# Mish in two instructions instead of one, shorter ends, and a new instruction order

## The chip, the cores and the metric

The kernel runs on one core of a Trainium2 chip. TensorE (PE), VectorE (DVE), ScalarE (ACT), GpSimd (POOL) and the DMA queues of SyncE (SP) and ScalarE work side by side and meet at semaphores. The metric is the time of one execution on the device in microseconds; lower is better.

## The reference

One input x of 2048 rows and 640 columns goes through two branches that a gate mixes row by row: full softmax attention with 32 heads of 20 columns, and a dense layer with Mish.

```
g = sigmoid((x * gate_w).sum(-1, keepdims=True))
qkv = x @ wqkv                       # 640 -> 3 * 640, 32 heads of 20
p = softmax(q @ k^T * 20**-0.5)      # 2048 x 2048 for each head
a = (p @ v) @ wo
h = x @ w1 + b1                      # 640 -> 1536
b = (h * tanh(log1p(exp(-|h|)) + max(h, 0))) @ w2     # Mish, 1536 -> 640
out = g * a + (1 - g) * b
```

The inputs are bfloat16.

## The kernel before

**Groups and units.** Attention runs in 32 groups: four heads (one row group of PE for each) by 512 queries. A group has 16 sets, one for each block of 128 keys, and a set has four units, one for each head. A unit is one score matmul (`score`, L1262): 32 x 128 keys against 32 x 512 queries, into one PSUM bank. So there are 2048 units.

**Two ways to an exponential.** Most sets go to ScalarE: `emit_exp` (L1312) takes the banks of two or three units in one instruction and writes to the ring `E`. Some sets go to VectorE instead (the planner calls one such set `d`): `power_of` (L473) makes a power of two from each bank by one multiply-add into 16-bit integers, and two further copies of the set, moved by whole numbers (`SHIFT`), are added up with fitting factors `VD` to better the approximation. These copies are made by VectorE (`shift`, L604, one instruction) or by GpSimd (`part`, L572, four instructions). The products with the values (`emit_pv`, L1355) gather into one bank, `acc`, with a column of ones for the row sums. At a group's end `normalise` transposes that bank (L1376), takes reciprocals (L1390), multiplies on GpSimd (L1397) and sends the result through DRAM.

**The other work.** Products that must be done some time during the attention are *chains* with a start and a due time: the q, k and v products (`xT,ws`, `wv,xT`), h = x @ w1 (`h_chain`, evacuated with the bias at L891), the Mish products (`b_chain`, `w_sb,big`) and the product with wo (`wo_chain`, `wo_sb,od`, evacuated at L1064). All of them go out through line L637, four column tiles side by side.

**Mish.** The hidden layer is done in two batches of 1024 rows. `mish` (L909 to L925) counts the finished pairs of h and then queues one ScalarE instruction over 12288 elements a partition. Exp and Mish need different tables, so each batch has a table load before it and one after it. A b product of the batch may begin when the instruction is done (`act_ready`).

**Who sets the order.** The schedule is fixed when the program is built. A planner keeps a model clock for each engine, and at each step lets `step_pe`, `step_act`, `step_dve` and `step_pool` choose the next instruction by rules (`rule`), whose settings change as the work advances (`PLAN`). The program then runs on the chip in just this order on every engine, and semaphores hold an engine where data are not there yet. At most two exps are under way at a time (`NOUT`), and seven banks are shared by scores and chains.

**Heat.** `heat`, in `step_pe`, lets the planner's PE pass one matmul's time when its recent activity is low. It emits no instruction.

**Start.** Before the loop the first 512 rows of x are loaded and transposed (L1454), `wkp` and `wqp` are put together from the loaded weights (`w_first`, `w_top`), and the first k and q are made (L1478), each into one bank, from which VectorE copies one half and ScalarE the other (L1486, L1487).

**End.** After the loop the last four row blocks get the rest of their product (L1830) and are copied out by ScalarE (L1845, L1852) and VectorE (L1854), and stored by SP's queue (L1848, L1856).

Of the kernel before, what the change touches and what calls it, by code (L numbers as in the profile page):

```python
# [9 lines left out]
P = 128  # L10
ACT = mybir.ActivationFunctionType
# [44 lines left out]
SWITCH = 100.0  # L56
# [8 lines left out]
def kernel(  # L65
# [249 lines left out]
    for u in range(NU):  # L315
        eng = nc.sync if u % 2 == 0 else nc.scalar
        eng.dma_start(out=xs[0][:, u, :], in_=x2d[u * P : (u + 1) * P, :])
    load_first(1, nc.sync)
    load_first(0, nc.scalar)
    nc.sync.dma_start(out=w_top[:, :, :], in_=wrows[:, :, D + KTOP : 2 * D])  # L320
    nc.scalar.dma_start(out=wv0[:, :, 0 : 4 * DH], in_=wrows[:, :, 2 * D : 2 * D + 4 * DH])

# [68 lines left out]
    pool_q = []  # L391
    two_port = [0.0]
    seq = [0]
    free = {"PE": 0.0, "ACT": 0.0, "DVE": 0.0, "POOL": 0.0}
# [514 lines left out]
    def mish(m, t):  # L909

        h_left[m] -= 1
        if h_left[m]:
            return
        lo = (m * MB % 2) * (FT // 2)
        v = big[:, lo : lo + MB * FT // 2, :].rearrange("p a b -> p (a b)")

        def done(t):
            for c in range(m * MB, m * MB + MB):
                for k in range(FT // 2):
                    act_ready[(c, k)] = t  # L920

        act_q.append((
            t, 2.0 * TABLE + 100.0 + MB * FT * 427.0,
            lambda t: nc.scalar.activation(v, v, ACT.Mish), done,  # L924
        ))  # L925

# [442 lines left out]
    def normalise(G, ready):  # L1369
# [3 lines left out]

        def a(t):
            st["T1"] = work.tile([P, NS, 32], F32, tag=f"T1_{i}", name="T1")
            nc.vector.transpose(out=st["T1"][:, :, :].rearrange("p b r -> p (b r)"), in_=acc[:, :])  # L1376
# [31 lines left out]
        def ends(t):  # L1408
            st["O"] = work.tile([P, QC], BF16, tag=f"O{i}", name="O")
            for h in range(2):  # L1410
                q = slice(h * QC // 2, (h + 1) * QC // 2)
                b_ = slice(h * NS // 2, (h + 1) * NS // 2)
                nc.vector.tensor_tensor(
                    out=T2[i][:, q].rearrange("p (b r) -> p b r", r=32)[:, :, 0:DH],
                    in0=st["T1"][:, b_, 0:DH],
                    in1=st["rec"][:, b_].unsqueeze(2).to_broadcast([P, NS // 2, DH]),
                    op=ALU.mult,
                )
                nc.vector.transpose(out=st["O"][:, q], in_=T2[i][:, q])
            o_last[p] = st["O"]  # L1420

        def c_done(t):
# [49 lines left out]
    pad_copy(nc.vector, wqp, w_first[0][:, :, :])  # L1472
    sb = [bank_ap(g, [P, QC]) for g in (6, 2)]
    kT[0] = kTb[0]
    qT[0] = qTb[0]
    for w, dst, k in ((wkp, kT[0][:, 0:QC], 0), (wqp, qT[0][:, :], 1)):
        for kt in range(KT):
            nc.tensor.matmul(  # L1478
                sb[k][:, :],
                lhsT=w[:, kt, :, :].rearrange("p h d -> p (h d)"),  # L1480
                rhs=xT[:, kt, 0:QC],
                start=(kt == 0),
                stop=(kt == KT - 1),
            )
        h_ = QC // 2
        nc.vector.tensor_copy(out=dst[:, 0:h_], in_=sb[k][:, 0:h_])  # L1486
        nc.scalar.copy(out=dst[:, h_:QC], in_=sb[k][:, h_:QC])  # L1487
    for p in range(NQ - NSB, NQ):
# [72 lines left out]
    work_log = deque()  # L1561
    heats = [0]

# [8 lines left out]
    def step_pe(t):  # L1572
# [34 lines left out]
        def go_f():  # L1607
# [4 lines left out]
            return sw + cost  # L1612

        def heat(room):

            cost = switch("V") + MM
            if pv_G[0] >= NG or acc_free[0] > t or activity(t) > rule.HEAT or not pv_done[pv_G[0]]:
                return None
            if cost + SWITCH + rule.HROOM > room:
                return None  # L1620
            enter("V")
            note(t, MM, 1.0)
            heats[0] += 1
            return cost

# [91 lines left out]
        if mode[0] in ("V", "F") and slack < rule.SWTH and not (stuck_ or end):  # L1717
            return d_alone(rule.DQ3) or heat(room)
        if n_pv and (n_pv >= rule.VMIN or tight or last_of_group) and (
# [5 lines left out]
        if n_pv and (n_pv >= rule.VMIN or tight or last_of_group or end):  # L1725
            return go_v()
        return d_alone(rule.DQ4) or heat(room)

# [11 lines left out]
    def step_dve(t):  # L1740
        best = None
        for it in dve_q:
            if it[1] <= t and (it[6] is None or it[6](t)):
                due = it[1] + (WAIT0, rule.WAIT1, rule.WAIT2, MWAIT)[it[0]]
# [99 lines left out]
    for u in range(2):  # L1844
# [3 lines left out]
        nc.sync.dma_start(out=rows_[u], in_=ots_[u][:, :])  # L1848
    for u, half, eng in ((2, 0, 0), (2, 1, 0), (3, 0, 0), (3, 1, 1)):
        dst, src = ots_[u][:, half * HALF : (half + 1) * HALF], places[u][half][:, 0:HALF]  # L1850
        if eng:
            nc.scalar.copy(out=dst, in_=src)  # L1852
        else:
            nc.vector.tensor_copy(out=dst, in_=src)  # L1854
        if half:
            nc.sync.dma_start(out=rows_[u], in_=ots_[u][:, :])  # L1856
    if DEBUG:
        print("model end us", t / 1e3, "last exp", last_exp[0] / 1e3, {k: v / 1e3 for k, v in idle.items()}, "sets", sum(n_d), n_d, "heats", heats[0])

# [29 lines left out]
```

## Time and profile before

Three runs took 721.22, 722.08 and 722.51 us.

| | us |
|---|---|
| median of the runs | 722.08 |
| the profiled execution | 722.37 |
| its span, first to last instruction | 720.6 |
| ACT busy | 700.0 |
| PE busy | 704.9 |
| DVE busy | 631.6 |
| POOL busy | 418.1 |
| exps on ScalarE, 710 instructions, busy | 668.8 |
| Mish, 2 instructions, busy | 20.9 |
| first score | 10.20 |
| end of the last exp | 711.85 |

Busy time is the union of an engine's instructions. Matmuls overlap and their ends are modelled, so PE's 98% says less than the starts of its instructions do. The mean of one exp is larger than the time from one exp to the next, since exps overlap as well.

The chain that ended last is made up of PE for 66% of the span and of ACT for 25%; by line, exps 24%, scores 23%, chains 21%, value products 21%. It changes between the two engines all the time: a score round waits for banks that an exp sets free, and an exp waits for a score round.

### The profile page before, as it was taken

The page shows a single profiled execution, that of the slowest core. Times are in us where ns is not written, and L with a number is a line of the kernel's source. Part 1 is how long each engine was busy: PE and PEld are TensorE (multiplying, and loading weights), DVE is VectorE, ACT ScalarE, POOL GpSimd, SP SyncE. Part 2 cuts the span into 40 slices and gives each one's busy share as a digit, 9 for nine tenths or more (in the row PEclk, how much of TensorE's full clock was granted, in tenths as well). Part 3 has the DMA queues.
Part 4 walks back from the last instruction along what each step waited for, and adds up shares of the span by engine and source line. Part 5 has one row for each costly group of instructions (what it writes and reads, how often), then busy time and mean ns, then how long its engine had stood idle before and what let it go on. Part 6 is the DMA issues. An engine that isn't in the chain of part 4 may idle for free.

```text
span 720.6 us, 24680 instructions
## 1 busy us (share of the span) xinstructions
PE 704.9 (98%) x10262; PEld 230.7 (32%) x10262; DVE 631.6 (88%) x1062; ACT 700.0 (97%) x726; POOL 418.1 (58%) x669
## 2 busy tenths in 40 slices
PE   7999999999999999999999999999989999999997
PEld 3433332222222333333333222222223333333333
DVE  4499998968868889999999998999998989999996
ACT  6899999999999999999999999999989999999996
POOL 2002864557868776877676687867964486762000
PEclk9999999999999999999999999999989999999999
DMA  9611122132322211111230223212211131131301
GB/s 249 180 24 33 31 47 52 34 69 57 80 43 51 50 29 17 23 32 28 46 92 25 46 51 84 65 43 43 60 20 30 33 68 27 31 63 15 61 20 47
DMA packets 123312, 37.86 MB, mean 53 GB/s; under 512 B 90880, under 2 KB 122640, under 8 KB 123200
## 3 DMA queue, kind: packets, MB, share of 16 engines
q1 hardware_dynamic: 121600, 35.76, 22.8%
q8 instruction: 80, 1.31, 0.8%
q10 hardware_dynamic: 1600, 0.53, 0.3%
q14 instruction: 32, 0.26, 0.2%
HBM read 22.29 MB, written 11.48 MB: 47 GB/s over the span
## 4 chain that ended last, share of the span: by engine, by line
PE 66%; ACT 25%; issue 5%; DVE 2%; DMA 1%; SPq 0%; POOL 0%; DVEq 0%; ACTq 0%
ACT E L1312 24%; PE Sp L1262 23%; PE Sp L637 21%; PE Sp L1355 21%; DVE T L473 1%; ACT big L924 1%; DMA w_top<-in_A_wqkv_dram 1%; PE Sp L1830 0%; DMA qT<-q_dram 0%; PE Sp L1478 0%; DVE T L604 0%; DMA q_dram<-st 0%; ACT L1312 0%; ACT L924 0%; DVE st L741 0%
## 5 line engine op out<-in xcount | busy, mean ns | idle before, releaser
L1312 ACT ACTIVATE E<-Sp 128x1024 bf16<-128x1024 f32 x710 | 668.8, 1079 | 6.8 <-PE Sp L1262 6.4
L572 POOL TENSOR_TENSOR T<-T,step_t 128x256 int32<-128x256 int32 x624 | 389.3, 659 | 108.0 <-PE Sp L1355 83.4
L473 DVE TENSOR_SCALAR T<-Sp 128x512 int16<-128x512 f32 (+1 forms) x595 | 391.9, 686 | 52.4 <-PE Sp L1262 46.3
L1262 PE MATMUL Sp<-qT,kT 32*128 32x512 bf16 x2048 | 288.3, 385 | 6.4 <-ACT E L1312 1.8
L1262 PEld LDWEIGHTS <-kT 32*128 32x128 bf16 x2048 | 74.2, 91 | 264.2 <-issue 260.0
L1355 PE MATMUL Sp<-E,VA 128*21 128x512 bf16 x1448 | 138.2, 383 | 0.0
L1397 POOL TENSOR_TENSOR T<-T,rec 128x320 bf16<-128x320 f32 x31 | 24.6, 792 | 164.9 <-DVE rec L1390 140.8
L604 DVE TENSOR_SCALAR T<-T 128x2048 int16<-128x2048 int16 x144 | 117.2, 819 | 1.4 <-PE Sp L1355 0.4
L1355 PE MATMUL Sp<-T,VD 128*21 128x512 bf16 x1200 | 113.5, 383 | 1.3 <-DVE T L604 1.3
L637 PE MATMUL Sp<-w_sb,big 128*32 128x320 bf16 x1536 | 79.4, 306 | 0.0
L637 PE MATMUL Sp<-xT,w1t 128*32 128x512 bf16 x960 | 76.6, 383 | 0.0
L1355 PEld LDWEIGHTS <-VA 128*21 128x21 bf16 x2048 | 45.2, 90 | 74.9 <-issue 67.3
L1355 PE MATMUL Sp<-T,VA 128*21 128x512 bf16 x600 | 58.2, 384 | 0.0
L637 PE MATMUL Sp<-xT,ws 128*32 128x512 bf16 x720 | 54.8, 382 | 0.2 <-DVE T L473 0.2
L637 PEld LDWEIGHTS <-big 128*32 128x32 bf16 x1536 | 34.8, 96 | 28.1 <-issue 18.5
L1355 PEld LDWEIGHTS <-VD 128*21 128x21 bf16 x1200 | 28.9, 90 | 37.5 <-issue 32.7
L891 DVE TENSOR_SCALAR big<-Sp,b1f 128x512 bf16<-128x512 f32 x48 | 35.6, 741 | 0.5 <-PE Sp L637 0.2
L637 PE MATMUL Sp<-wv,xT 128*32 128x81 bf16 (+2 forms) x960 | 33.0, 258 | 1.0 <-DVE T L473 1.0
L637 PE MATMUL Sp<-wo_sb,od 128*32 128x320 bf16 (+1 forms) x608 | 32.6, 302 | 0.0
L637 PEld LDWEIGHTS <-w1t 128*32 128x32 bf16 x960 | 19.6, 94 | 26.3 <-issue 21.2
L741 DVE CAST st<-Sp 128x512 bf16<-128x512 f32 x36 | 24.4, 681 | 3.8 <-PE Sp L637 3.3
L1376 DVE STREAM_TRANSPOSE T<-Sp 128x512 f32<-128x512 f32 x32 | 22.7, 709 | 2.1 <-PE Sp L1355 1.8
(74 smaller groups left out, 198.2 us busy)
## 6 DMA issues: line engine op xcount, KB each, us to landing
w1t<-in_B_w_dram SPq DMA_DIRECT2D x24, 320.0 KB
q_dram<-st SPq DMA_DIRECT2D x20, 128.0 KB
out_dram<-ot SPq DMA_DIRECT2D x16, 160.0 KB
qT<-q_dram SPq DMA_DIRECT2D x124, 20.0 KB
o_dram<-T SPq DMA_DIRECT2D x120, 20.0 KB
kT<-k_dram SPq DMA_DIRECT2D x28, 80.0 KB
k_dram<-st SPq DMA_DIRECT2D x16, 128.0 KB
big<-in_A_x_dram SPq DMA_DIRECT2D x3, 640.0 KB
```

What stands on the lines that cost most here:

```text
L473: nc.vector.tensor_scalar(out=dst.bitcast(I16), in0=src, scalar1=inv_sqrt_dh * LOG2E * 128.0, scalar2=127.0 * 128.0 + BETA, op0=ALU.mult, ...
L572: nc.gpsimd.tensor_tensor(out=tile_[:, :].bitcast(I32)[:, k * n : (k + 1) * n], in0=d["T"][:, :].bitcast(I32)[:, k * n : (k + 1) * n], in1 ...
L604: nc.vector.tensor_scalar(out=tile_[:, :].bitcast(I16), in0=d["T"][:, :].bitcast(I16), scalar1=float(SHIFT[i]), scalar2=None, op0=ALU.add,)
L637: nc.tensor.matmul(out_[k : k + 32], lhsT=lhsT[:, k : k + 32], rhs=rhs, tile_position=(0, k), **kw)
L741: nc.vector.tensor_copy(out=res["st"][:, :], in_=ps[:, :])
L891: nc.vector.tensor_scalar(out=big[:, slot.tag, (ft % 2) * QC : (ft % 2 + 1) * QC], in0=ps[:, :], scalar1=b1f[:, ft : ft + 1], scalar2=None ...
L924: lambda t: nc.scalar.activation(v, v, ACT.Mish), done,
L1262: nc.tensor.matmul(ps_cols, lhsT=kT[p][32 * t_ : 32 * t_ + 32, j * P : (j + 1) * P], rhs=qT[G][32 * t_ : 32 * t_ + 32, :], tile_position=( ...
L1312: nc.scalar.activation(E[:, x : x + n, :], ps, ACT.Exp, scale=inv_sqrt_dh,)
L1355: nc.tensor.matmul(acc[32 * t_ : 32 * t_ + DH + 1, :], lhsT=lhsT, rhs=rhs, start=(pv_done[G] == 0), stop=(pv_done[G] == pv_total[G] - 1), ...
L1376: nc.vector.transpose(out=st["T1"][:, :, :].rearrange("p b r -> p (b r)"), in_=acc[:, :])
L1397: nc.gpsimd.tensor_tensor(out=T2[i][:, :].rearrange("p (b r) -> p b r", r=32)[:, :, 0:DH], in0=st["T1"][:, :, 0:DH], in1=st["rec"][:, :].u ...
```

## The change

It has four parts.

- **Mish.** Each batch becomes two instructions of 512 rows (6144 elements a partition), one behind the other. The planner takes the first half's results as there one half earlier, and the b products of those 512 rows may be placed then.
- **The start.** `w_top` is loaded by ScalarE's queue as its third load, ahead of the q weights; the first v weights go to SP's queue in its place. The first k and q products are made in two halves of 256 columns, in banks 1 and 4, and 5 and 0, so that VectorE and ScalarE copy from different banks.
- **The end.** While the last group is normalised (`closing`), VectorE takes only work of the highest kind. Of the last copies ScalarE makes three whole row blocks and VectorE the two halves of the other; the stores keep their order.
- **The planner.** `heat` is taken out. The rules and `PLAN` are the same; since the costs of Mish and the steps differ, the planner comes to another order of the instructions on all engines after the first two groups.

```diff
+    nc.scalar.dma_start(out=w_top[:, :, :], in_=wrows[:, :, D + KTOP : 2 * D])
     load_first(0, nc.scalar)
-    nc.sync.dma_start(out=w_top[:, :, :], in_=wrows[:, :, D + KTOP : 2 * D])
-    nc.scalar.dma_start(out=wv0[:, :, 0 : 4 * DH], in_=wrows[:, :, 2 * D : 2 * D + 4 * DH])
+    nc.sync.dma_start(out=wv0[:, :, 0 : 4 * DH], in_=wrows[:, :, 2 * D : 2 * D + 4 * DH])
...
-        lo = (m * MB % 2) * (FT // 2)
-        v = big[:, lo : lo + MB * FT // 2, :].rearrange("p a b -> p (a b)")
+        one = 200.0 + FT * 427.0
 
         def done(t):
+            for k_, c in enumerate(range(m * MB, m * MB + MB)):
+                for k in range(FT // 2):
+                    act_ready[(c, k)] = t - TABLE - (MB - 1 - k_) * one
+
+        def run(t):
             for c in range(m * MB, m * MB + MB):
-                for k in range(FT // 2):
-                    act_ready[(c, k)] = t
-
-        act_q.append((
-            t, 2.0 * TABLE + 100.0 + MB * FT * 427.0,
-            lambda t: nc.scalar.activation(v, v, ACT.Mish), done,
-        ))
+                lo = (c % 2) * (FT // 2)
+                v = big[:, lo : lo + FT // 2, :].rearrange("p a b -> p (a b)")
+                nc.scalar.activation(v, v, ACT.Mish)
+
+        act_q.append((t, 2.0 * TABLE + MB * one, run, done))
...
+            closing[0] = G == NG - 1
...
             o_last[p] = st["O"]
+            closing[0] = False
...
-    sb = [bank_ap(g, [P, QC]) for g in (6, 2)]
-    for w, dst, k in ((wkp, kT[0][:, 0:QC], 0), (wqp, qT[0][:, :], 1)):
+    h_ = QC // 2
+    for w, dst, two in ((wkp, kT[0], (1, 4)), (wqp, qT[0], (5, 0))):
         for kt in range(KT):
-            nc.tensor.matmul(
-                sb[k][:, :],
-                lhsT=w[:, kt, :, :].rearrange("p h d -> p (h d)"),
-                rhs=xT[:, kt, 0:QC],
-                start=(kt == 0),
-                stop=(kt == KT - 1),
-            )
-        h_ = QC // 2
-        nc.vector.tensor_copy(out=dst[:, 0:h_], in_=sb[k][:, 0:h_])
-        nc.scalar.copy(out=dst[:, h_:QC], in_=sb[k][:, h_:QC])
+            for h in range(2):
+                nc.tensor.matmul(
+                    allb[:, two[h], 0:h_],
+                    lhsT=w[:, kt, :, :].rearrange("p h d -> p (h d)"),
+                    rhs=xT[:, kt, h * h_ : (h + 1) * h_],
+                    start=(kt == 0),
+                    stop=(kt == KT - 1),
+                )
+        nc.vector.tensor_copy(out=dst[:, 0:h_], in_=allb[:, two[0], 0:h_])
+        nc.scalar.copy(out=dst[:, h_:QC], in_=allb[:, two[1], 0:h_])
...
-        def heat(room):
-
-            cost = switch("V") + MM
-            if pv_G[0] >= NG or acc_free[0] > t or activity(t) > rule.HEAT or not pv_done[pv_G[0]]:
-                return None
-            if cost + SWITCH + rule.HROOM > room:
-                return None
-            enter("V")
-            note(t, MM, 1.0)
-            heats[0] += 1
-            return cost
...
-            return d_alone(rule.DQ3) or heat(room)
+            return d_alone(rule.DQ3)
...
-        return d_alone(rule.DQ4) or heat(room)
+        return d_alone(rule.DQ4)
...
-            if it[1] <= t and (it[6] is None or it[6](t)):
+            if it[1] <= t and (it[0] == 0 or not closing[0]) and (it[6] is None or it[6](t)):
...
-    for u, half, eng in ((2, 0, 0), (2, 1, 0), (3, 0, 0), (3, 1, 1)):
-        dst, src = ots_[u][:, half * HALF : (half + 1) * HALF], places[u][half][:, 0:HALF]
-        if eng:
-            nc.scalar.copy(out=dst, in_=src)
-        else:
-            nc.vector.tensor_copy(out=dst, in_=src)
-        if half:
-            nc.sync.dma_start(out=rows_[u], in_=ots_[u][:, :])
+    nc.scalar.copy(
+        out=ots_[3][:, :].rearrange("p (a c) -> p a c", a=2), in_=allb[:, 6:8, 0:HALF]
+    )
+    for half in range(2):
+        nc.vector.tensor_copy(
+            out=ots_[2][:, half * HALF : (half + 1) * HALF], in_=places[2][half][:, 0:HALF]
+        )
+    for u in (2, 3):
+        nc.sync.dma_start(out=rows_[u], in_=ots_[u][:, :])
```

More of the change, by code (lines that the diff above doesn't have):

```diff
@@ L392 @@
     two_port = [0.0]
+    closing = [False]
     seq = [0]
@@ L1561 @@
     work_log = deque()
-    heats = [0]
     def note(t, cost, weight):
@@ L1848 @@
         nc.sync.dma_start(out=rows_[u], in_=ots_[u][:, :])
-    for u, half, eng in ((2, 0, 0), (2, 1, 0), (3, 0, 0), (3, 1, 1)):
-        dst, src = ots_[u][:, half * HALF : (half + 1) * HALF], places[u][half][:, 0:HALF]
-        if eng:
-            nc.scalar.copy(out=dst, in_=src)
-        else:
-            nc.vector.tensor_copy(out=dst, in_=src)
-        if half:
-            nc.sync.dma_start(out=rows_[u], in_=ots_[u][:, :])
+    nc.scalar.copy(
[7 more added lines that the diff above has]
+        nc.sync.dma_start(out=rows_[u], in_=ots_[u][:, :])
     if DEBUG:
-        print("model end us", t / 1e3, "last exp", last_exp[0] / 1e3, {k: v / 1e3 for k, v in idle.items()}, "sets", sum(n_d), n_d, "heats", heats[0])
+        print("model end us", t / 1e3, "last exp", last_exp[0] / 1e3, {k: v / 1e3 for k, v in idle.items()}, "sets", sum(n_d), n_d)
 _INS = ['A_x', 'A_wqkv', 'A_wo', 'B_x', 'B_w1', 'B_b1', 'B_w2', 'gate_w']
```

## The prediction

> **What bounds the kernel now.** I read the page's engine line first, then ACT's groups with their shapes kept apart.
>
> ```profile
> span 720.6 us, 24680 instructions
> ...
> PE 704.9 (98%) x10262; PEld 230.7 (32%) x10262; DVE 631.6 (88%) x1062; ACT 700.0 (97%) x726; POOL 418.1 (58%) x669
> ...
> PEclk9999999999999999999999999999989999999999
> ```
>
> ```profile
> L1312 ACT ACTIVATE E<-Sp 128x1024 bf16<-128x1024 f32 x682 | 635.5, 1061 | 6.8 <-PE Sp L1262 6.4
> L1312 ACT ACTIVATE E<-Sp 128x1536 bf16<-128x1536 f32 x28 | 42.2, 1507 | 0.0
> L924 ACT ACTIVATE big<-big 128x12288 bf16<-128x12288 bf16 x2 | 20.9, 10444 | 0.0
> L924 ACT ACT_TABLE_LOAD x2 | 2.6, 1283 | 0.0
> ```
>
> Two engines are full, ACT and PE. Between the first exp at 10.62 us and the end of the last at 711.85, ACT stands visibly idle for only 6.8 us. Exps overlap: five in a row take 4.69 us in the timeline at 235.62, so one starts (4.69 - 1.06) / 4 = 0.907 after the other. By the same overlap of 0.154 a three-bank exp costs 1.507 - 0.154 = 1.35. ACT's own work there is 682 x 0.907 + 28 x 1.35 + 20.9 + four table loads 5.1 = 682, against 701 elapsed; some 19 us are waiting, most in lags too short to count as idle. PE is read from its starts:
>
> ```profile
> 305.78 0.39 PE L1262 MATMUL Sp<-qT,kT 32*128 32x512 bf16 x3
> 306.10 0.59 PE L637 MATMUL Sp<-w_sb,big 128*32 128x320 bf16 x12
> 306.62 0.39 PE L1262 MATMUL Sp<-qT,kT 32*128 32x512 bf16 x3
> ```
>
> A score round costs 0.32 until the column-tiled work begins. That work streams four tiles side by side: 12/4 x 320 columns at 2.4 a ns = 0.40, then 0.12 passes before the next round. Summed so from first to last score of the program, PE needs about 677 of 699 us. Neither engine has room of more than 3%, so both sums must be taken for the changed order too.
>
> **The place the change aims at** is the second Mish. Timeline of ACT, then of PE, then windows (us from:to, length, PE busy, PEld, DVE, ACT, POOL, granted clock, DMA share, GB/s):
>
> ```profile
> 519.98 10.44 ACT L924 ACTIVATE big<-big 128x12288 bf16<-128x12288 bf16 x1
> 530.44 1.28 ACT L1312 ACT_TABLE_LOAD   x1
> 531.74 1.94 ACT L1312 ACTIVATE E<-Sp 128x1024 bf16<-128x1024 f32 x2
> 535.27 1.02 ACT L1312 ACTIVATE E<-Sp 128x1024 bf16<-128x1024 f32 x1 [1.60 <-PE Sp L1262]
> 536.67 3.94 ACT L1312 ACTIVATE E<-Sp 128x1024 bf16<-128x1024 f32 x4 [0.38 <-PE Sp L1262]
> ```
>
> ```profile
> 526.33 0.40 PE L1355 MATMUL Sp<-T,VD 128*21 128x512 bf16 x4 [1.31 <-DVE T L604]
> ...
> 532.58 2.06 PE L637 MATMUL Sp<-w_sb,big 128*32 128x320 bf16 x28
> ```
>
> ```profile
> 526.20:529.60 3.40, 2.85 (x17) 0.74 (x17) 3.40 (x7) 3.40 (x1) 0.00 (x0) 0.99 0.11 39
> 529.60:533.00 3.40, 3.18 (x21) 0.70 (x23) 3.40 (x7) 3.37 (x4) 2.90 (x5) 0.50 0.22 15
> 533.00:536.40 3.40, 3.40 (x46) 1.14 (x34) 2.25 (x4) 1.70 (x2) 3.29 (x5) 0.50 0.15 9
> ```
>
> While ACT runs Mish no b product may start, the ready work runs out, and PE is left with single scores paced by DVE: 17 matmuls in the 3.4 us from 526.2, where the window after 536.4 has 60. From 529.6 to 536.4 the granted clock is 0.50. The first b products after Mish, 28 of them, then take 2.06 us instead of 28/4 x 0.133 + 0.12 = 1.05, and ACT waits 1.60 + 0.38 = 2.0. The first Mish (241.6) has no such loss: clock 1.00, busy PE, exp directly behind the table load.
>
> On that clock the Trainium skill (TensorE: Matmul & The Clock Gate, "Why this matters for your kernels") says that gaps without matmuls should stay under about 3 us, since one idle window puts the gate back to half rate. Here it fell though the longest gap was 1.31 us: sparse work was enough, so the measurement decides. By the page's rule a PE with such gaps would keep its clock, and the 2.0 us below would be no gain of a denser PE.
>
> **The change part by part**, against the profiled execution: 722.37 us, span 720.6 and 1.8 around it. The median of the runs is 722.08, 0.29 less; I take that off at the end.
>
> 1. *Start.* The last chain before the first score is:
>
> ```profile
> 6.60 0.22 DVE L1469 COPY wkp<-w_top 128x240 bf16<-128x240 bf16 x1 [0.55 <-DMA w_top<-in_A_wqkv_dram]
> 9.31 0.42 DVE L1486 CAST qT<-Sp 128x256 bf16<-128x256 f32 x1 [0.72 <-PE Sp L1478]
> 9.77 0.37 ACT L1487 CAST qT<-Sp 128x256 bf16<-128x256 f32 x1 [0.78 <-DVE qT L1486]
> 10.20 0.40 PE L1262 MATMUL Sp<-qT,kT 32*128 32x512 bf16 x4 [0.99 <-ACT qT L1487]
> ```
>
> The halves of k and q now lie in different banks, and in the changed program ACT's copy waits for PE only: 9.77 - 9.31 = 0.46 saved. w_top goes from fourth on SP's queue (issued 2.12) to third on ACT's (such an issue stood at 1.65): 0.47 earlier at most; nothing if the transfers still end together. Moved behind it, the q weights come perhaps 1 us later, but their copy is first needed some 1.2 us after the k product starts, which covers it; uncovered they would take the 0.47 back. What takes the place on SP's queue (the first v weights, 100 instead of 60 KB) delays the next x block by some 0.3 us; its transposes began at 10.53, after its landing. Twenty 256-column matmuls stream as many columns as ten of 512: between 0 and 0.2 more. Sum -0.9 (from -0.4 to -1.0). The first two groups stand in the same PE order afterwards, so it is carried on.
>
> 2. *Mish split.* Two more instructions; a 128x1 activation took 0.20, so 0 to 0.2 each: +0.4 of ACT. No table load is added (five before, five after), because no exp lies between the halves. The gain is in the second batch: the changed order gives PE, from the first half on, 48 and then 52 b products, a quarter of 0.133 each, so 1.6 and 1.7 us of dense work inside the second half, and an exp's scores are already there behind the table load. Work before them: 18 column-tiled steps of 0.22 and some rounds, about the 6.6 us of table load and half a Mish. So -2.0; between 0 (the wait returns) and -2.6 (the two lags after it too).
>
> 3. *The new order.* Both programs' instructions counted: exps of two banks 682 -> 693, of three 28 -> 23, of one 0 -> 1; score rounds 717 -> 711; column-tiled matmuls 8092 -> 8076; power sets on DVE 150 -> 148; shifts on DVE 144 -> 133, on POOL 156 -> 163 sets. ACT: 11 x 0.907 - 5 x 1.35 + 0.46 (half a two-bank exp; none in the trace; 0.2 to 0.9 by the 128x1 form and the two-bank one) + 0.4 = +4.1. PE: -6 x 0.44 - 16/4 x 0.213 = -3.5. DVE -8 x 0.60 - 11 x 0.68 = -12, hidden in its 90 us of idle; POOL +28 x 0.66 = 18, in its 300. The removed heat step emitted no instruction, so it costs nothing by itself.
>
> These sums are not spread evenly. Up to the last group (units 0 to 1983 of 2048) ACT has 657.2 -> 663.6, PE 654.9 -> 655.6; that stage took 677.1 before (10.2 to 687.3). Taking in each stretch of rounds the larger of the two sums, and averaging over where the cuts lie:
> stretches of 6 rounds: 676.7 -> 676.2; of 10: 672.1 -> 672.6; of 20 (a group): 667.0 -> 668.4; of 80: 662.0 -> 664.8.
> Ten is my choice: it leaves 5.0 of the 677.1 for waits outside both sums, and the trace names some 4 (2.0 after Mish; 0.6 behind a q load at 117; 0.8 on DVE at 42.3; about 0.5 at 430). So +0.5, from -0.5 (6 rounds) to +6.4 (all of ACT's sum). The other waits I take as replaced by as many.
>
> 4. *Last group.* From its first score to the closing transpose it took 712.36 - 687.3 = 25.1. Now ACT has 21.2, PE 19.4 to its last score, but DVE, packed until 707 before, has 23.5 up to its last shift, plus 0.5 for the product behind it: 24.0 if packed, 25.3 with a wait like the 1.45 before. I take 24.6: -0.5 (-1.1 to +0.2).
>
> 5. *Closing.* Other evacuations are held back during the last normalisation: the one at 712.99 put the reciprocal 0.36 later; -0.4. The copies at the very end now stand two on DVE, three on ACT. Third on ACT would end about 1.9 after the first starts; SP issues the four stores 0.47 apart from 0.7 on, so the fourth at 2.1 hides it. Without that cover it costs 0.2.
>
> Sum: -0.9 - 2.0 + 0.5 - 0.5 - 0.4 = -3.3; 722.37 - 3.3 - 0.29 = **718.8**.
>
> **Rivals.**
> *ACT's sum comes through.* If PE is no longer what is late, each stretch costs what ACT has: +6.4 instead of +0.5, so 724.7. It is one mechanism, ScalarE from group 2 to 30, and decides from the point where PE's rounds leave exps always ready. For: ACT is 97% busy and gets the larger sum over long stretches. Against: in most groups before, the elapsed time was within 0.3 of the larger sum and that was PE's more often than ACT's. Slower.
> *The wait moves.* The clock falls again, or a q load or a shift is late elsewhere by as much: 718.8 + 2.0 = 720.8, no change. For: during the first half PE still has single scores paced by DVE at 0.6 each. Against: this thin spell lasts some 3 us, before it lasted 8; and b products follow.
> *The order fits better.* Short waits shrink too: by stretches of 6, whose sum nearly reaches the 677.1, -0.5 in place of +0.5, with the last group at -1.1 and 0.6 for the q load gone: 716.6.
> *The split does nothing*, the b products stand behind other work and begin after both halves: the order counted above speaks against it; it would give 720.8 as well, and is counted with the second.
>
> **Numbers.** Forecast 0.50 (own range 717.3 to 720.6), ACT's sum 0.16, the wait moves 0.20, fits better 0.14. About 0.2%, 1.4 us, is what a measurement here tells from no change: faster is under 720.6, slower over 723.5. Faster 0.47 + 0.14 + a third of 0.20 = 0.67; slower 0.12 from ACT's sum (the rest of it falls short of 723.5); same 0.21. The range 715.8 to 723.8 leaves out most of ACT's case above 723.8 and a little below.
>
> **What would show it.** Right: the first score at about 9.3; granted clock 1.00 through the second Mish and an exp within 0.2 behind its table load; group 31 DVE packed to its end; reciprocal directly behind the closing transpose. Wrong: idle of ACT behind score rounds well over 6.8 us; a clock of 0.50 in the middle; or ACT starting exps 0.907 apart nearly throughout while the time grows.

## The result, and the profile after

The changed kernel takes 724.63 us (median of 6 runs, 723.72 to 725.96), the kernel before, run beside it, 722.30 (6 runs, 721.22 to 722.95). The ratio is 1.0032, with a 95% interval from 1.0017 to 1.0047: some 2.3 us slower. Forecast were 718.8 and 3.3 us faster. In the profiled executions the span went from 720.6 to 723.2.

The page of the changed kernel, then ACT's groups with their shapes kept apart:

```profile
span 723.2 us, 24705 instructions
...
PE 706.3 (98%) x10256; PEld 232.5 (32%) x10256; DVE 619.6 (86%) x1042; ACT 704.3 (97%) x735; POOL 430.4 (60%) x697
...
PEclk9999999999999999999999999999999999999999
```

```profile
L1315 ACT ACTIVATE E<-Sp 128x1024 bf16<-128x1024 f32 x693 | 644.4, 1064 | 6.2 <-PE Sp L1265 5.9 <-PE Sp L1358 0.2
L1315 ACT ACTIVATE E<-Sp 128x1536 bf16<-128x1536 f32 x23 | 34.2, 1487 | 0.1
L926 ACT ACTIVATE big<-big 128x6144 bf16<-128x6144 bf16 x4 | 21.1, 5315 | 0.0
```

In this execution the clock is whole up to the last matmul, where before it dipped in the middle (in two of the six runs the mean clock is 0.997 instead of 0.999, about one fall of 3.4 us at 0.50). Nothing on this page looks worse, and both busy shares stand as they were. Where the time went is seen only by stage. A group (64 units) is counted from the first score round that holds no score of the group before:

| us | before | after | the stage's change | forecast |
|---|---|---|---|---|
| first score | 10.2 | 9.2 | -1.0 | -0.9 |
| group 1 | 39.7 | 40.7 | +2.0 | 0 |
| group 5 | 126.1 | 126.7 | -0.4 | } |
| group 23 (second Mish) | 511.5 | 515.8 | +3.7 | } -1.5 |
| group 24 | 543.7 | 546.6 | -1.4 | } together |
| group 31 (the last) | 687.3 | 692.2 | +2.0 | } |
| closing transpose | 712.4 | 715.5 | -1.8 | -0.5 |
| end of the span | 720.6 | 723.2 | -0.5 | -0.4 |

(-1.5 is -2.0 for the Mish and +0.5 for the order.) A round can straddle two groups, so a stage holds some scores more or fewer: group 23 holds 67 before and 63 after, groups 24 to 30 hold 445 and 449. At about 0.34 us a score (561.2 us for 1662) that is 1.4 us, as much as the -1.4 of group 23. Over groups 1 to 30 the two kernels differ by one score. So two stages lost: the first group, and the long stretch of groups that holds neither end nor the second Mish.

**The second Mish does what was forecast.** Windows in its second half, then ACT's timeline:

```profile
528.10:531.50 3.40, 3.17 (x39) 1.08 (x35) 3.40 (x6) 3.40 (x1) 3.40 (x7) 1.00 0.41 58
531.50:535.00 3.50, 3.46 (x100) 2.55 (x100) 2.39 (x4) 3.50 (x2) 3.44 (x6) 1.00 0.13 20
```

```profile
531.58 5.31 ACT L926 ACTIVATE big<-big 128x6144 bf16<-128x6144 bf16 x1
536.91 1.28 ACT L1315 ACT_TABLE_LOAD   x1
538.20 4.69 ACT L1315 ACTIVATE E<-Sp 128x1024 bf16<-128x1024 f32 x5
```

PE has 39 and then 100 matmuls in the second half, at clock 1.00, and five exps follow the table load without a wait.

**The first group loses the start again.** SP's queue after, then before (start, length of the issues, count):

```profile
19.83 4.44 SPq L1500 DMA_DIRECT2D o_dram<-wo  x4
24.38 5.14 SPq L708 DMA_DIRECT2D k_dram<-kT  x4
29.61 0.35 SPq L745 DMA_DIRECT2D q_dram<-st  x1
30.06 2.60 SPq L708 DMA_DIRECT2D k_dram<-kT  x4
32.76 1.39 SPq L780 DMA_DIRECT2D qT<-q_dram  x4
```

```profile
19.50 3.20 SPq L1495 DMA_DIRECT2D o_dram<-wo  x4
...
31.14 1.39 SPq L779 DMA_DIRECT2D qT<-q_dram  x4
```

The second q tile is loaded 1.6 us later than before, though the first score is 1.0 earlier. The queue is full: its issues stand one behind the other, and the four zero stores hold it for 4.44 us instead of 3.20. PE then waits:

```profile
33.98 0.39 PE L1265 MATMUL Sp<-qT,kT 32*128 32x512 bf16 x2
35.21 0.71 PE L1265 MATMUL Sp<-qT,kT 32*128 32x512 bf16 x2 [0.84 <-DMA qT<-q_dram]
```

Set against the kernel before, whose order on PE is the same in this group, 1.6 of the 2.0 us are lost at this load; the other 0.4 go at the transposes at 18.14 us, where the trace names no releaser. The loss is that of one profile. In a_heat, a_p1 and a_p2 (below), with the same order on PE in the first group, the load is issued at 30.57, 31.09 and 33.23, and group 1 begins at 39.2, 40.0 and 41.1.

**The long stretch waits for banks.** PE's waits, after and then before (us in all, times, longest):

```profile
PE Sp L1265 <- ACT E L1315: 3.7, 12, 0.5
PE Sp L638 <- DVE T L474: 1.7, 4, 1.0
```

```profile
PE Sp L1262 <- ACT E L1312: 1.8, 6, 0.5
PE Sp L1355 <- DVE T L604: 1.3, 1, 1.3
...
PE Sp L637 <- DVE T L473: 1.2, 2, 1.0
```

These lines hold the whole program, and the 1.3 us before stand in the second Mish; over groups 5 to 30 alone the waits for exps are 2.9 us in 9 after and 0.6 in 2 before. They count only time in which PE stands visibly idle. Counted from start to start, with 0.32 us for up to four scores, 0.216 for each four more, and 0.053 for a column-tiled product of 512 columns and 0.12 for a passage to the next round, the time above that price over groups 5 to 30 is 15.2 us before and 19.2 after. In rounds of two scores it fell from 2.8 to 1.0 (three of the second Mish's waits among them), in rounds of four it rose from 1.7 to 4.7, and five rounds of five to seven scores, a form that the order before doesn't have there, add 4.2. One of them stands behind the first Mish:

```profile
255.90 0.39 PE L1265 MATMUL Sp<-qT,kT 32*128 32x512 bf16 x2
256.62 0.37 PE L1265 MATMUL Sp<-qT,kT 32*128 32x512 bf16 x1 [0.33 <-DVE bt L975]
257.21 0.37 PE L1265 MATMUL Sp<-qT,kT 32*128 32x512 bf16 x1 [0.22 <-DVE T L474]
258.06 0.39 PE L1265 MATMUL Sp<-qT,kT 32*128 32x512 bf16 x2 [0.47 <-ACT E L1315]
```

Six scores that would take 0.54 take 2.5. Three times the round waits for a bank that another engine has not emptied, and the products that stand behind it in PE's order wait too.

### The profile page after: what moved, and what is told of

The parts are those of the page before. It is cut to its first block, busy times and chain, and to the rows that moved or that the text cites. A ratio compares the mean times of both kernels' runs of the same rounds, so it can differ in the third digit from the quotient of the medians.

```text
span 723.2 us, 24705 instructions
## 1 busy us (share of the span) xinstructions
PE 706.3 (98%) x10256; PEld 232.5 (32%) x10256; DVE 619.6 (86%) x1042; ACT 704.3 (97%) x735; POOL 430.4 (60%) x697
## 4 chain that ended last, share of the span: by engine, by line
PE 62%; ACT 23%; issue 5%; DVE 4%; SPq 2%; DMA 2%; POOL 0%; ACTq 0%; POOLq 0%
PE Sp L1265 22%; ACT E L1315 20%; PE Sp L1358 20%; PE Sp L638 20%; DVE T L474 2%; ACT big L926 1%; DMA w_sb<-in_B_w_dram 1%; DVE T L605 1%; SPq L291 1%; SPq L304 1%; DMA big<-in_A_x_dram 1%; PE Sp L1822 0%; SPq L708 0%; SPq L324 0%; ACT L1315 0%
## 5 line engine op out<-in xcount | busy, mean ns | idle before, releaser
L573 POOL TENSOR_TENSOR T<-T,step_t 128x256 int32<-128x256 int32 x652 | 401.1, 649 | 107.9 <-PE Sp L1358 71.5
L605 DVE TENSOR_SCALAR T<-T 128x2048 int16<-128x2048 int16 x133 | 105.2, 797 | 1.5 <-PE Sp L1358 0.5
L638 PE MATMUL Sp<-w_sb,big 128*32 128x320 bf16 x1536 | 74.3, 301 | 0.3 <-DVE st L742 0.3
L1358 PEld LDWEIGHTS <-VD 128*21 128x21 bf16 x1184 | 28.4, 90 | 37.6 <-issue 32.2
L638 PE MATMUL Sp<-wv,xT 128*32 128x81 bf16 (+2 forms) x960 | 34.6, 258 | 1.3 <-DVE T L474 1.3
L826 DVE CAST VA<-Sp 128x80 bf16<-128x80 f32 (+2 forms) x48 | 16.2, 372 | 10.1 <-PE Sp L638 10.1
```

What stands on the lines that cost most here:

```text
L573: nc.gpsimd.tensor_tensor(out=tile_[:, :].bitcast(I32)[:, k * n : (k + 1) * n], in0=d["T"][:, :].bitcast(I32)[:, k * n : (k + 1) * n], in1 ...
L605: nc.vector.tensor_scalar(out=tile_[:, :].bitcast(I16), in0=d["T"][:, :].bitcast(I16), scalar1=float(SHIFT[i]), scalar2=None, op0=ALU.add,)
L638: nc.tensor.matmul(out_[k : k + 32], lhsT=lhsT[:, k : k + 32], rhs=rhs, tile_position=(0, k), **kw)
L826: nc.vector.tensor_copy(out=VA[:, sts[i], h0 : h0 + nh, 0:DH], in_=ps[:, i, 0:n].rearrange("p (h d) -> p h d", d=DH),)
L1358: nc.tensor.matmul(acc[32 * t_ : 32 * t_ + DH + 1, :], lhsT=lhsT, rhs=rhs, start=(pv_done[G] == 0), stop=(pv_done[G] == pv_total[G] - 1), ...
```

## The experiments

"1→31" is the time from the start of group 1 to that of group 31, counted as above: 647.6 before, 651.5 after.

### The two ends

*b_ends*: the kernel before with the changed start and end alone.

> The kernel before with the two shortened ends alone (w_top's queue, the k and q halves, the closing, the last copies); its order from first score to last group is that of the kernel before. Theory (the start's gain is taken back, because the q load of the second group stands behind bulk loads in SP's queue, whose pace doesn't follow PE): first score at 9.2 to 9.3, but the second group begins no earlier than before, 39.7 or later, and the whole is 0 to 0.6 faster than before, by the closing alone. Rival (the start's gain is carried on, and what the changed kernel lost there came from its order): second group at 38.8, whole 1.0 to 1.5 faster.

Measured: 724.48 us (8 runs), ratio 1.0043 (1.0025 to 1.0061); span 722.3. The second group begins at 40.0, as the theory had it, but the whole is slower and not faster. Group 31 begins 0.3 earlier than before, and the end comes 1.7 later. In the order of before one evacuation of the wo product isn't due until the last normalisation, and `closing` holds it back. VectorE, then PE:

```profile
714.39 0.45 DVE L1421 STREAM_TRANSPOSE O<-T 128x256 bf16<-128x256 bf16 x1
714.75 0.51 DVE L1065 SCALAR_TENSOR_TENSOR big<-Sp,g_t,xT 128x320 bf16<-128x320 f32 x1
```

```profile
715.32 0.43 PE L1833 MATMUL Sp<-wo,O 128*128 128x320 bf16 x2 [1.82 <-DVE big L1065]
```

So the closing rule is worth -0.4 only with an order that has all evacuations done by then, as the changed kernel's; with another it costs more than the rest of both ends saves.

*a_lz*: the changed kernel with the four zero stores (`o_dram`) issued behind the gate values instead of before the loop.

```diff
-    for u in range(NU):
-        nc.sync.dma_start(out=o_dram...)
...
+        for u in range(NU):
+            nc.sync.dma_start(out=o_dram...)
         nc.sync.dma_start(out=g_dram[:, :], in_=g_t[:, :])
```

> The changed kernel with the four stores of zeros to o_dram (3 to 4.5 us of SP's queue, ahead of the q load of the second group) put behind the gate's values, some 10 us later; the order of the compute engines is the same. Theory (the start's gain is lost in SP's queue): the second group begins at 38.2 to 39.2 instead of 40.7, the whole is 1.0 to 2.0 faster than the changed kernel, so 722.6 to 723.6. Rival (the load is late by the transfers themselves, or PE waits there for VectorE): second group at 40.5 or later, no change.

Measured: the q load is issued at 29.95 instead of 32.76 and the second group starts at 39.2 instead of 40.7, so the load's place in the queue was the cause; group 10 starts at 234.1 instead of 235.7. But the median is 724.93, ratio to before 1.0042 (1.0025 to 1.0059): nothing of it arrives, and the expected whole was missed. Windows behind the first Mish:

```profile
254.70:258.10 3.40, 2.37 (x29) 0.82 (x30) 3.29 (x6) 3.39 (x4) 2.41 (x5) 1.00 0.13 45
258.10:261.50 3.40, 3.40 (x46) 1.14 (x38) 2.33 (x4) 2.66 (x4) 2.67 (x4) 0.50 0.02 5
```

The six waiting scores of above now lie 1.55 us earlier, the granted clock falls to 0.50 for 3.4 us behind them, and the 1.5 us are gone by group 11 (267.4 against 267.5). All four runs have a mean clock of 0.996 to 0.997. The changed kernel has the same 29 matmuls in the 3.4 us from 256.20, with the same 2.37 us of PE busy, and keeps its clock, so the long round alone does not decide whether it falls.

*b_head_lz*: the kernel before with the changed start and the late zero stores; its own end, order and Mish.

> The kernel before with the change's start alone and the four stores of zeros put behind the gate's values; end and order as before. Theory (the start saves 0.6 to 1.0 once the q load isn't late, and the closing was what made the two ends slower): second group at 38.7 to 39.2, last group's start 0.5 to 1.4 earlier than before unless the clock falls at the first Mish, whole 720.6 to 721.5. Rival (the start's halves cost later what they save): 722 or more.

Measured: 721.26 us (10 runs), the kernel before beside it 721.99 (19 runs), ratio 0.9989 (0.9979 to 0.9998). The lead is 0.5 at group 1, 1.0 from group 5 (the q load at 117 is no longer late) and 1.1 at the end of the span. The expectation was met in all three points. Of the versions that compute everything it is the only one that beats both kernels, and by little.

### Mish alone, and the clock

*b_split_emit*: the kernel before, order unchanged, with each Mish emitted as two instructions.

```diff
-            lambda t: nc.scalar.activation(v, v, ACT.Mish), done,
+            lambda t: [nc.scalar.activation(w_, w_, ACT.Mish) for w_ in halves], done,
```

> The kernel before with each Mish issued as two instructions and nothing else: the planner reckons as before, so every other instruction stands where it stood. Theory (the loss comes with the new order, and the gain at the second Mish needs b products that are placed in its second half): granted clock 0.50 again behind the second Mish, wait of ACT there about 2, whole 0 to +0.4. Rival (the split itself is costly or itself saves the wait): more than +1, or -1.5 or better with the clock at 1.00.

Measured: 722.52 (10 runs), before 721.98 (17 runs), ratio 1.0006 (0.9996 to 1.0015). The two halves take 10.54 us instead of 10.44, and the clock falls as before (0.50 from 529.9). The split brings something only through the order that it lets the planner make.

*b_realheat*: the kernel before, in which each heat step emits four matmuls with zero weights into the accumulating bank. *b_head_lz_heat*: b_head_lz with such heats in the second half of the run alone.

```diff
             heats[0] += 1
+            for k in range(4):
+                nc.tensor.matmul(
+                    acc[32 * k : 32 * k + DH + 1, :], lhsT=zero_w[:, 0 : DH + 1], rhs=w2_sb[:, 0, 0:QC],
+                    start=False, stop=False, tile_position=(0, 32 * k),
+                )
```

> The kernel before in which the planner's heat step emits what it reckons with: four column-tiled matmuls of zero weights into the open group's sums, 28 times in all, 10 of them in the second Mish; every other instruction stands as before. Theory (the wait after the second Mish is the clock's: sparse scores let it fall): granted clock 1.00 to the end, no idle of ACT over 0.3 behind that Mish, whole 1.5 to 2.2 faster, 719.8 to 720.5, the other 18 hidden. Rival (the wait is for b products and banks, and the clock only falls along with it): the wait stays at 1 or more, whole no faster.

> The kernel before with the start part of the change, the zero stores behind the gate values, and the planner's heat steps of the second half emitting four matmuls with zero weights into the accumulating bank, so that PE stays busier around the second Mish. Order otherwise that of before. Theory (the start is worth 1.0 once the q load is not late, and the fall of the clock behind the second Mish costs about 1.4 more, of which the heats give back 1.4): 719.9. Rival (heats cost PE as much as they save): 721.3, as without them.

Measured: b_realheat 723.25 (10 runs), ratio 1.0030 (1.0012 to 1.0047). In its profile the clock stays at 1.00, ACT's wait behind the second Mish is 0.6 instead of 2.0, and group 23, with the same scores in it, takes 30.8 instead of 32.2 us; but the early heats cost 0.9 in the first group and 0.9 more by group 5. Four of its ten runs have a mean clock of only 0.992 to 0.993. The expected gain of 1.5 to 2.2 us was missed. b_head_lz_heat 721.57 (11 runs), ratio 1.0000 (0.9981 to 1.0019): against b_head_lz it loses 0.8 at the first Mish and 0.5 more up to group 23, and gains 1.3 there. Its expectation of 719.9 was missed, the rival's 721.3 hit. Denser PE work at the second Mish is worth 1.3 to 1.4 us, and costs as much elsewhere.

### What the new order waits for

*a_heat*: the changed kernel with the heat step back in the planner, so a third order.

> The changed kernel with the planner's heat step put back, which emits nothing, so that the order comes out anew: ACT's sum over groups 1 to 30 is 634.5 (636.5 in the changed kernel, 630.1 in the kernel before), PE's 626.3 (629.4, 628.7), the larger of the two by group 641.2 (639.7, 636.5). Theory (ACT's sum comes through in these groups): they take about 2 less than the changed kernel's 651.5, so 649.5. Rival (the larger sum of each group counts): 1.5 more, 653.

Measured: 727.1 and 727.3 us in two runs with a mean clock of 0.999 and 1.000, 735.9 and 739.2 in two with 0.992 and 0.985; without the last the ratio is 1.0115 (1.0053 to 1.0178). In the profile, at 727.1, 1→31 took 653.7, ACT's sum being 2.0 less than in the changed kernel. Time does not follow ACT's sum. Nor is it the missing heat that costs: with it back the stretch takes 2.2 us more.

*b_short*, *a_short*: both kernels with each exp over 480 of 512 columns. *b_half*, *a_half*: over 256. *b_cut*, *a_cut*: over 256, and the powers on VectorE too.

```diff
-            E[:, x : x + n, :], ps, ACT.Exp, scale=inv_sqrt_dh,
+            E[:, x : x + n, 0:256], ps[:, :, 0:256], ACT.Exp, scale=inv_sqrt_dh,
...
-                    power_of(d["T"][:, r * QC : (r + 1) * QC], ps[:, :])
+                    power_of(d["T"][:, r * QC : r * QC + 256], ps[:, 0:256])
```

> The kernel before with every exp of ScalarE cut to 480 of its bank's 512 columns (the last 32 queries of a bank are left out and read as ones; a two-bank exp is then about 0.053 shorter, ACT's sum 37 less), same order. ACT is now far from being the bound: groups 1 to 30 should take PE's sum of 628.7 and 6 to 14 more. To be compared with the next run.

> The changed kernel with the same cut of every exp, same order as the changed kernel. PE's sum over groups 1 to 30 is 629.4, 0.7 more than in the run above. Theory (the order's loss of 3.9, or 5.9 with the clock's 2.0 set aside, is that ACT has more to do in these groups): the two cut kernels differ by less than 1.5 there, the clock set aside. Rival (the loss is in waits of the new order for banks, for VectorE or for loads): they still differ by 3 or more.

> The kernel before with every exp cut to the first 256 of its 512 columns (the rest of the ring E is filled with ones once), order unchanged. An exp becomes about half a microsecond shorter, so a bank comes free that much sooner. It is the other half of the next run's comparison. All theories: groups 1 to 31 take 644.8 (the run with 480 columns) or up to 4 us less, since PE's own sum with fixed costs is 628.7 and VectorE's waits stay.

> The changed kernel with the same cut to 256 columns. Theory (the new order loses its time where a score round must wait for a bank that an exp still holds, 7 such waits of 4.5 us in the changed kernel against 1 of 0.6): with exps half a microsecond shorter these waits nearly vanish, and of the 5.2 us by which the changed kernel is longer over groups 1 to 31 with 480 columns at most 2 are left. Rival (VectorE's powers and evacuations, or PE's own sum, are what the new order waits for): the difference stays at 4 to 6 us. ACT's own sum can't matter in either run.

> The kernel before with exps and powers both cut to 256 of 512 columns (the rest of E and of the tiles of the powers filled with ones once); order unchanged. Banks come free sooner on ScalarE and on VectorE alike. It is the other half of the next run's comparison; where no clock falls, its groups should come near PE's own sum, 628.7 us over groups 1 to 30, plus the waits at the second Mish.

> The changed kernel with the same two cuts. Theory (the new order loses its time because score rounds and value products wait for banks and tiles, for ScalarE's exps and VectorE's powers together): with both shortened the waits inside score rounds nearly go, and over stretches in which neither kernel's clock falls the changed kernel is at most 1 us longer over groups 5 to 30 (it was 4.3 whole, 2.5 with the exps alone cut; PE's own sums differ by 0.7 over groups 1 to 30). Rival (the time lies in PE's own order, switches between forms or passages): 2.5 stays.

The medians were 718.43 and 725.38 (one run each), 721.06 and 719.00 (8 and 3 runs), 715.31 and 716.22 (2 each). They hold falls of the clock that come at different places (b_half lost nearly 4 us to one in group 4), so groups 5 to 30 are compared, with and without group 23, in which the clock falls in all four runs with the order of before:

| groups 5 to 30, us | order of before | changed order | difference | without group 23 |
|---|---|---|---|---|
| whole | 561.2 | 565.6 | 4.3 | 5.7 |
| exps 480 | 559.7 | 564.4 | 4.7 | 6.4 |
| exps 256 | 558.7 | 561.2 | 2.5 | 4.2 |
| exps and powers 256 | 554.5 | 555.5 | 1.0 | 2.4 |

The stretches without group 23 hold 1595 scores before and 1600 after, but by the prices above 520.5 and 518.9 us of PE work, since more of the chains lie in group 23 after. The pair with 480 includes a fall of the clock at 259.7 to 263.1 in the changed order, behind the six scores; group 10, which holds it, takes 33.2 us there instead of 31.8, so without it that pair differs by some 3.3 or 5.0. Over 1→31 that pair took 644.8 and 650.0: the theory that ACT has more to do (less than 1.5 apart) fails. What an exp costs with 256 columns, in the changed kernel:

```profile
L1316 ACT ACTIVATE E<-Sp 128x512 bf16<-128x512 f32 x693 | 412.7, 597 | 227.1 <-PE Sp L1266 223.8 <-PE Sp L1359 0.4
```

With 227 us of idle before the two-bank exps ACT bounds nothing, and still 4.2 us remain: its sum is not the cause. But an exp that lasts 597 instead of 1064 ns frees its banks sooner: waits inside score rounds that an exp ended fell from 7 (4.5 us) to 5 (1.1 us). The bound of 2 us that this theory set was missed, though. With the powers shortened as well the difference is 2.4, or 1.0 with group 23, just on the bound set for that pair, and the five long rounds stand 1.5 us above their price instead of 4.2. So shorter exps and powers take away 3.3 of the 5.7 us. That they do so by freeing banks fits these rounds; the runs do not part it from the two engines' smaller sums, beyond the pair with 480, where ACT's busy time is 18.5 us smaller and at most 1.0 goes. What is left is not PE's price, which is smaller after; it stands in score rounds of three and more again, over groups 5 to 30 7.3 us above their price against 3.3 in b_cut. Passages that the trace names "issue" (1.5 us), what is left of the powers (1.3) and exps (1.3) and evacuations that were not cut (1.3) share it; how, stays open. Of the expectations for the order of before, b_short's was missed (1→31 took 644.8, 16 above PE's sum and not 6 to 14) and b_half's as well (647.6, with the fall in group 4); b_cut took 638.1, 9.4 above PE's sum, some 5.5 of it in group 23.

*a_p1*, *a_p2*: the changed kernel with only the planner's fixed cost of half a Mish at 100 and 300 ns instead of 200. *b_p1*: the kernel before with that of a whole one at 300 instead of 100. Each program is the same as its parent up to the first Mish, and ordered anew behind it.

```diff
-        one = 200.0 + FT * 427.0
+        one = 100.0 + FT * 427.0
```

> The changed kernel with only the planner's fixed cost of half a Mish changed from 200 to 100 ns: the program is the same up to the first Mish (group 10), and the planner comes to another order behind it. Theory (time differs from order to order by the waits that happen to arise, by as much as the change's own parts are worth): groups 10 to 31 differ from the changed kernel's by 1 to 4 us in either direction. Rival (any order with the split Mish and these rules costs what ACT's and PE's sums make it, some 651.5 over groups 1 to 31): within 0.7 us of it.

> The changed kernel with the planner's fixed cost of half a Mish at 300 instead of 200 ns: a second other order behind the first Mish. Theory (order to order the time differs by more than the parts of the change are worth; 100 ns gave 739): anything from 722 to 745, and not within 0.7 us of the changed kernel. Rival (100 ns was one accident, orders by these rules lie close together): 723.5 to 725.5.

> The kernel before with only the planner's fixed cost of a Mish changed from 100 to 300 ns: the order is the same up to the first Mish and another one behind it; Mish stays one instruction. Theory (the settings of the rules fit the one order they stand with, so that any other order behind them costs more, with or without the split): 2 us or more longer than before. Rival (only orders with the split Mish lose): within 1 us of before.

| groups 1 to 30, us | PE's sum | larger sum, by group | 1→31 measured | median of the runs |
|---|---|---|---|---|
| before | 628.7 | 636.5 | 647.6 | 722.3 |
| after | 629.4 | 639.7 | 651.5 | 724.6 |
| b_p1 | 627.7 | 642.8 | 650.8 | 728.1 |
| a_p2 | 627.4 | 638.4 | 651.5 | 726.3 |
| a_heat | 626.3 | 641.2 | 653.7 | 727.3 |
| a_p1 | 628.2 | 637.5 | 664.9 | 739.0 |

(a_heat's median leaves out its slowest run. The second column moves by up to 2 us with where a group is cut.) The ratios to before are 1.0222 (1.0208 to 1.0236) for a_p1, 1.0062 (1.0047 to 1.0077) for a_p2, 1.0091 (1.0074 to 1.0108) for b_p1. PE's sums lie within 3.1 us, the measured times within 17, and the second column does not rank them either. b_p1 loses without the split, so a new order is enough for a loss. a_p2's median lies in the range expected, but its 1→31 is the changed kernel's own. a_p1 is far outside the 1 to 4 us expected: from 505.8 to 511.8 PE makes 76 products of h and q with 8 value products between them and no score, at a granted clock of 0.66 in the 5 us from 505 on, and ACT stands idle for 8.66 us:

```profile
512.65 5.68 ACT L1315 ACTIVATE E<-Sp 128x1024 bf16<-128x1024 f32 x6 [8.66 <-PE Sp L1358]
```

Groups 22 and 23 together take 7.6 us more than in the changed kernel. Group 24 takes another 7.0 more, and there it is a load: VectorE waits 6.13 us for `bl` until 568.65, PE 5.20 us for VectorE's evacuation, and the clock falls for 6.83 us from 566.66. So an order can lose to a load as well as to banks.

## Why the prediction was wrong

**What bounds it.** Two full engines were read rightly, but "both sums must be taken" led astray. In the changed kernel, halving the exps takes 241 us of busy time from ACT (704.3 to 463.5) and 4.3 us from groups 5 to 30. PE's fixed order, with the banks that it waits for, is the bound there, and ACT's 97% is the echo of it.

**1, start.** The first score came at 9.24 (-1.0 for -0.9):

```profile
9.24 0.40 PE L1265 MATMUL Sp<-qT,kT 32*128 32x512 bf16 x4 [0.46 <-ACT qT L1492]
```

That is the favourable end: nine profiles with this start and no cut in the exps below 480 columns have it at 9.17 to 9.75, five with the start of before at 10.11 to 10.40. The step that failed is "so it is carried on": PE's order is indeed the same in the first group, but the q load of the second tile hangs on SP's queue. The prediction followed the queues that the moved loads pass only up to the first score. a_lz and b_head_lz show the queue as the cause: with the zero stores behind it the load is issued at 29.5 to 30.0, and group 1 begins at 39.2. Cost in the profile: 2.0 us, 1.6 of them at the load; in other profiles of this first group from 0.1 (a_heat) to 2.4 (a_p2).

**2, Mish split.** Right: clock 1.00, no wait behind the table load. Above the larger of its two sums group 23 stood 2.9 us before and 0.4 after, so -2.5 for the -2.0 forecast; its length alone (30.8 instead of 32.2) is no measure, as it holds four scores fewer. The Trainium skill (TensorE: Matmul & The Clock Gate, "Why this matters for your kernels") asks for idle gaps under about 3 us; in a_lz that was not enough, since there the clock fell behind a stretch whose longest idle time of PE was 0.48 us.

**3, the new order.** The term that decided: +0.5 forecast. Groups 1 to 30 took 3.9 us more with the second Mish's -2.5 in them, so the rest of the order cost about +6.4 (+5.3 with group 23 taken by its length). Taken group by group the larger of both sums rises by 3.2 (636.5 to 639.7), which looks like the answer; but with exps over 480 columns ACT's busy time is 18.5 us smaller in the changed kernel (704.3 to 685.8), and of the difference at most 1.0 goes with it, and the measure fails for the other orders of the table above. What failed is the step "the other waits I take as replaced by as many", an assumption without a row behind it. The changed order waits 19.2 instead of 15.2 us over groups 5 to 30 although group 23's share fell from some 6.6 to 3.5, and the added waits are in score rounds of four and more. The long rounds could have been counted in the changed order before any run: in groups 5 to 30, five of five to seven scores against none.

**4, last group.** Right in direction, too small: 23.2 us instead of 24.6. VectorE is packed from the group's start to the shift before the closing transpose, as forecast, but its work and the product behind it come to 0.8 less than the 24.0 that were added up. Some 0.3 of that is the group's mark, which lies one score late; which row was too dear stays open.

**5, closing.** Right: from the closing transpose to the end 7.7 instead of 8.2, the reciprocal directly behind it:

```profile
715.46 0.72 DVE L1380 STREAM_TRANSPOSE T<-Sp 128x512 f32<-128x512 f32 x1 [0.50 <-PE Sp L1358]
716.21 0.25 DVE L1394 RECIPROCAL rec<-T 128x16 f32<-128x16 f32 x1
```

b_ends shows the condition that was not named: the order must have no evacuation left.

**The rivals.** "ACT's sum comes through" gave 724.7, within 0.1 of the median, and is still not what happened: that number is luck. With ACT idle for 227 us in a_half 2.5 to 4.2 us of the difference remain, and a_heat takes longer with less on ACT. "The wait moves" came nearest: the waits moved, but from the one place to many, and grew. The chances rested on a sum of busy times which, by the six orders above, says little within 17 us.

## What to carry to other kernels

Where engines run a fixed order, sums of busy time give a floor and not a forecast: read the new order for rounds in which one engine takes several buffers in a row with nothing in between, for that is where the others' latency comes out. A planner's settings that are made stage by stage seem to fit the one order that they stand with: in all five other orders tried here, each from a small edit, the stretch took 3.2 to 17.3 us longer, so a local gain of 2 us is better made with the order kept, as the start was in b_head_lz. And a step that starts earlier gains only if each queue it passes still serves the next consumer in time.

## What the runs showed of the hardware

*The clock falls on sparse work, and not in every run of a program.* It falls in pieces of 3.41 us: 6.83 us behind the second Mish before, with 17 matmuls in the 3.4 us ahead, and 3.41 in a_lz, with 29. The changed kernel kept 1.00 behind 39 in its second Mish, and behind the very 29 of a_lz, which lie 1.55 us later there. Of b_head_lz_heat's 11 runs seven had a mean granted clock of 0.999 to 1.000 and took 720.5 to 721.8 us, four had 0.992 to 0.993 and took 724.8 to 725.9, with the same instructions in the same order. Three of a_heat's runs took 727.1 (0.999), 727.3 (1.000) and 735.9 (0.992). By the Trainium skill (TensorE: Matmul & The Clock Gate, "What's actually happening") the window in which activity is judged is about 3.4 us long and runs free of the program's start; the lengths of the falls and their coming and going agree with that.

*The same DMA issue holds its queue for different times.* The first of the four zero stores took 1.67 to 3.56 us of SP's queue in the fifteen profiles that issue it at 19 to 20 us, 1.67 before and 1.84 after, and 0.36 in the three that issue it at 41 us. What sets it is not shown.
